# Infini-attention with a SiLU feed-forward: the first query block's mask moved from TensorE to VectorE, and the planned order redrawn

## The chip, the cores and the metric

The kernel runs on one core of a Trainium2 chip. The metric is the device time of one execution in microseconds (us). A core has a matrix engine (TensorE, PE in the profile), with a unit that loads its stationary operand (PEld), a vector engine (VectorE, DVE), an activation engine (ScalarE, ACT), a general engine (GpSimd, POOL) and a queue engine that starts transfers (SyncE, SP). Each engine works through its own instructions in a fixed order, and waits on semaphores where it needs another engine's result. Matrix products land in PSUM, which the kernel uses as eight banks of 128 partitions by 512 fp32.

## The reference

The input `x` has 2048 tokens of width 448. Two branches are mixed by a gate for each token:

```python
q, k, v = x @ wq, x @ wk, x @ wv          # 16 heads of 28, 4 segments of 512 tokens
for s in range(4):                        # for each head
    logits = qs @ ks.T * scale + mask     # causal within the segment
    a_dot = softmax(logits) @ vs
    a_mem = (phi(qs) @ M) / (phi(qs) @ z + 1e-6)
    o = sigmoid(beta) * a_mem + (1 - sigmoid(beta)) * a_dot
    M += phi(ks).T @ vs;  z += phi(ks).sum()
a = concat(o) @ wo
b = silu(x @ w1) @ w2                     # width 1792
g = sigmoid((x * gate_w).sum(-1))
out = g * a + (1 - g) * b
```

`phi` is x + 1 above zero and exp(x) below. `wq` and `wk` come 200 times larger than an ordinary draw, so the softmax needs the true maximum of each row, and the products need more than fp16's precision.

## The kernel before, in words

Each fp32 operand is split into an fp16 part and the fp16 rest, called hi and lo, and a product is made of three products (hi·hi, lo·hi, hi·lo). The work falls into 16 groups, numbered t = 0 to 15: four heads of one segment each.

The first stage, until about 150 us, is `project()`: products for q, k and v (line 632 with `wqs`, `wks`, `wvs`), the sums of the memory M and z (line 1050 and 1052 on TensorE into a `cc` bank; line 1061 on VectorE reduces them into the buffer `md`; line 1064 on GpSimd scales them by `bds` into `macc`; lines 1069 and 1070 make the hi and lo of `macc`), and the retrieval from memory (lines 1087 to 1093). The `bds` and many other scale factors of one to a few columns are made by GpSimd in short instructions (lines 530 and 532), grouped into tasks by a helper, `few`.

The second stage, until about 472 us, mixes two things. One is the attention of 64 heads. For each group, `maxima` first finds the largest score of each row: lines 733 and 737 make scores in an `sc` bank, lines 742 and 747 reduce them on VectorE, line 755 transposes the result. The first query block of a group (128 rows for four heads, 128x512 in one bank) gets its causal mask from TensorE: line 733 multiplies an identity by the mask with start=True, and line 737 adds the four heads' scores on top; line 742 then reduces. For the other blocks line 747 adds the mask and reduces in one instruction. Then, for each head, line 1353 makes the scores again, transposed and with the maximum subtracted; line 1358 (ScalarE) takes exp; lines 1361 and 1364 (GpSimd) clear what lies above the diagonal; line 1370 (ScalarE) makes the hi half; line 1374 (GpSimd, three instructions) makes the lo half; line 1387 (TensorE, 20 matmuls) multiplies by v; line 1395 reduces. The other thing is the feed-forward's first ten of 14 chunks: line 632 with `wa` is the product with W1, lines 1236 and 1237 are a joint pass in which two chunks finish on the two halves of TensorE, lines 1209, 1211, 1213 and 1215 make SiLU and its hi and lo (`ghl`), and line 1257 is the product with W2.

The third stage, until the end, is the rest of the feed-forward and the product with `wo`, which must wait for the attention's output.

What stands where on each engine is decided when the kernel is built, by a list scheduler written in the kernel (`Sched`). It plans each task with a cost (`act`, `dve`, `pool`, `pe`, `few`; `half(512)` is 0.2165 us and `few(n)` is 0.33·n us), a latency from engine to engine, and a priority; among the tasks that can start it takes by priority. Buffers and PSUM banks go round in rings: three banks for `sc`, three for `mm`, two for `cc`, and after the first stage one of `cc`'s goes to `mm`. A task that takes a buffer is planned after its last user. The priorities come from some 35 constants at the head of the file. A planned cost is no instruction: it only moves the task's neighbours. On the chip the instructions keep the planned order and wait for what is late.

Of the names in the excerpts below, `mm_…`, `sc_…` and `cc_…` are tiles in PSUM banks, `mx` holds the maxima, `mk` the mask in fp32, `ring` q and k of a group.

Of the kernel before, what the change touches and what calls it, by code (L numbers as in the profile page):

```python
# [14 lines left out]
OP = mybir.AluOpType  # L15
# [15 lines left out]
TWINP = 30.0  # L31
TWO = 0.27
# [6 lines left out]
MORE = 6  # L39
HPRIO = 26.57  # L40
# [9 lines left out]
WOT = 258.31  # L50
# [3 lines left out]
LOP = 66.17  # L54
LATE = -0.07
FIRST = 104.6
WPRIO = 91.56
MAXO = 57.4
# [3 lines left out]
MP = 23.61  # L62
VF = -52.52
VA = 12.88
VS = 2.68
NV = 8
XH0 = -44.21
NF = 4
VE = 10.92
LASTQ = 6.3  # L70
WQS = -136.22
VH = 44.78
XS0 = -76.47
VC = -7.5
OT1 = -114.26
XS = 34.75
QS = -34.17
KS1 = -32.16
SS = -9.2
# [6 lines left out]
PRICE = 235.91  # L86
PRICE2 = 67.41
SLACK2 = 0.33
PVRUNS = [((1, 0), 1)]
PVP = 79.52  # L90
FLO = 50.28
FHI = 729.09
WOP = 8.33
SZ = 16.64
SZSTEP = 1.72
XPRIO = 345.51
WBP = 34.36
# [183 lines left out]
def infini_mix(ctx: ExitStack, tc: tile.TileContext, x, wq, wk, wv, wo, beta, w1, w2, out):  # L281
# [271 lines left out]
    def others(s, prio, bds, own, t_own, t_gh):  # L553

        def mem():
            z = spk[:, NSEG + s:NSEG + s + 1]
            by(z, top[:, WK:WK + 1], top[:, xi(s)], 1.0 / FIT)
            by(z, z, 1.0 / UP, op0=OP.max)
            by(bds[:, s, :, DH:], own[:, :, None], z[:GW])
            by(bds[:, s, :, :DH], own[:, :, None].to_broadcast([GW, 4, DH]), z[:GW], rv[:GW, s:s + 1])  # L560

        def go():
            by(rv[:, s:s + 1], top[:, WV:WV + 1], top[:, xi(s)], 1.0 / FIT)
            by(omgs[:, s], omg, rv[:, s:s + 1])
# [12 lines left out]
        EREADY[s] = few(5, scores, PREADY[s], SCALED[WQ], SCALED[WK], prio=prio + 0.5)  # L577
        END1.append(EREADY[s])
# [3 lines left out]
    def derive(s, prio):  # L582
# [7 lines left out]
        return few(5, go, SCALED[W1], EREADY[s], GDONE[s], prio=prio)  # L590
# [122 lines left out]
    def maxima(t, o):  # L713
# [12 lines left out]
        for q, (i, hs) in enumerate(plan):  # L726
# [4 lines left out]
            def go(i=i, hs=hs, ps=ps, n=n):  # L731
                if i == 0:
                    nc.tensor.matmul(ps.v, identb, maskb[:, None, :].to_broadcast([128, 4, 128]), start=True,
                                     stop=False, skip_group_check=True)
                for j, hh in enumerate(hs):
                    u = j * n
                    nc.tensor.matmul(ps.v[:, u:u + n], rg.v[:KS, 0, hh, i * 128:(i + 1) * 128], rg.v[:KS, 1, hh, :n],  # L737
                                     start=(i > 0), stop=(i > 0 or j == 3), skip_group_check=(i == 0))

            def red(i=i, hs=hs, ps=ps, n=n):  # L740
                if i == 0:
                    nc.vector.tensor_reduce(mx.v[:, :, 0], ps.v.rearrange("p (h n) -> p h n", h=4), axis=AX.X,
                                            op=OP.max)
                    return
# [4 lines left out]
            m = pe((half(512) if i == 0 else []) + half(n, len(hs)), go, *rs, *MKS, takes=[ps], uses=[rg], prio=p0)  # L749
            reds.append(dve(len(hs) * (n + 184) if i else 512, red, m, *reds[:1], takes=[] if reds else [mx], uses=[ps, mx],  # L750
# [15 lines left out]
    def project():  # L766
# [22 lines left out]
        ring("md", [GW, 4, DH + 1], F32, 1)  # L789
# [59 lines left out]
        def xhalves(s, c, prio):  # L849
# [354 lines left out]
    def unit(s, fs, prio, finish, gate=(), tail=False):  # L1204
# [16 lines left out]
        for a, b in zip(own[::2], own[1::2] + [None]):  # L1221
# [11 lines left out]
            if b is not None:  # L1233
# [4 lines left out]
                m = pe([(TWO, 0.06)], both, *[h[5] for h in held], TWIN[s], uses=[x for h in held for x in (h[1], h[3])],  # L1238
# [304 lines left out]
```

## Time and profile before

| | before |
|---|---|
| median of three runs | 563.09 us (562.89 to 563.65) |
| the profiled execution | 563.36 us, span 561.4 us |
| mean granted clock of TensorE in it | 0.991 |
| busy TensorE, share of the span | 545.4 us, 97% |
| busy ScalarE | 408.7 us |
| busy VectorE | 397.9 us |
| busy GpSimd | 353.9 us |

The profiled execution's time is 1.96 us more than its span, which is the work between the first and the last instruction. In the views, a row gives start, duration, engine, line, operation, output<-input and shape; "x19" are 19 instructions in a row; brackets give the idle time of that engine just before, and what ended it. Matmuls overlap, so the pace of a row of equal ones is its time less one latency, over their count less one.

### The profile page before, as it was taken

Reading aid. Unit: us, or ns where it says so; the run is one execution under the profiler, and the core shown is the slowest. Engines: PE = TensorE matmul, PEld = TensorE weight load, DVE = VectorE, ACT = ScalarE, POOL = GpSimd, SP = SyncE. Lnnn points to the kernel's source line nnn. Section 1 sums busy time; section 2 is a strip of 40 time slices with the busy share of each in tenths; the row PEclk is TensorE's granted clock in tenths of the full one; section 3 lists DMA queues with packets and bytes.
Section 4 is the critical chain, followed back from the end, with each engine's and each line's share of the span. In section 5 each row is a group of like instructions: output and inputs, shape, how many; then the busy total and the mean of one; then the engine's idle time right before and its main releaser. Section 6 shows DMA issues by size and latency. Waiting matters only on the chain.

```text
span 561.4 us, 11595 instructions
## 1 busy us (share of the span) xinstructions
PE 545.4 (97%) x4044; PEld 297.1 (53%) x4044; DVE 397.9 (71%) x987; ACT 408.7 (73%) x700; POOL 353.9 (63%) x550
## 2 busy tenths in 40 slices
PE   9998999899999899999999999999999997999997
PEld 3445655556644455555565555665556553455544
DVE  5998889788668765688655888766885347764472
ACT  6978889576368878899887989789997996500140
POOL 3345354673405787888988988798999996211310
PEclk9999999999999799999999999999999999899999
DMA  8787767453485324322333333456301212689872
GB/s 307 238 242 214 229 192 202 143 179 111 149 225 157 101 60 125 103 84 72 98 94 91 85 87 103 127 143 137 103 19 53 84 51 58 227 210 223 247 190 82
DMA packets 78378, 79.19 MB, mean 141 GB/s; under 512 B 44232, under 2 KB 68040, under 8 KB 78320
## 3 DMA queue, kind: packets, MB, share of 16 engines
q1 hardware_dynamic: 77744, 77.47, 48.1%
q10 hardware_dynamic: 576, 0.99, 0.5%
q8 instruction: 31, 0.51, 0.4%
q14 instruction: 27, 0.22, 0.1%
HBM read 48.41 MB, written 26.09 MB: 133 GB/s over the span
## 4 chain that ended last, share of the span: by engine, by line
PE 63%; DVE 9%; ACT 9%; DMA 8%; POOL 5%; SPq 3%; issue 3%; POOLq 0%; DVEq 0%; ACTq 0%
PE mm L632 16%; PE mm L1257 15%; PE sc L1353 5%; PE sc L737 5%; PE cc L1387 5%; DMA ol<-o_scr 5%; PE sc L632 4%; PE cc L632 4%; PE cc L1257 4%; ACT pf L1358 1%; SPq L657 1%; POOL phl L1374 1%; DVE stg L938 1%; DMA xraw<-in_x_dram 1%; SPq L366 1%
## 5 line engine op out<-in xcount | busy, mean ns | idle before, releaser
L1374 POOL TENSOR_TENSOR phl<-pf,phl 128x384 f16<-128x384 f32 (+1 forms) x192 | 190.5, 1010 | 24.9 <-ACT phl L1370 24.8
L1358 ACT ACTIVATE pf<-sc,lift,es 128x512 f32<-128x512 f32 (+1 forms) x192 | 127.9, 708 | 16.0 <-PE sc L1353 13.6
L747 DVE CUSTOM_DVE_ANT_0 sc<-sc,mk 128x384 f32<-128x384 f32 (+1 forms) x192 | 105.6, 570 | 34.2 <-PE sc L737 32.5
L1257 PE MATMUL mm<-wb,ghl 128*128 128x448 f16 (+2 forms) x516 | 113.7, 352 | 0.0
L632 PE MATMUL mm<-xh,wa 128*128 128x512 f16 x393 | 100.7, 379 | 0.0
L1257 PEld LDWEIGHTS <-ghl 128*128 128x128 f16 x684 | 64.0, 98 | 54.0 <-issue 2.9
L1370 ACT ACTIVATE phl<-pf 128x1280 f16<-128x1280 f32 x64 | 81.3, 1272 | 13.8 <-POOL pf L1364 12.0
L632 PEld LDWEIGHTS <-wa 128*128 128x128 f16 x524 | 48.9, 98 | 52.6 <-issue 7.3
L1353 PE MATMUL sc<-ring 86*128 86x512 f16 (+3 forms) x256 | 62.7, 301 | 1.0 <-DVE mx L747 0.5
L737 PE MATMUL sc<-ring 84*128 84x128 f16 (+3 forms) x256 | 59.4, 303 | 1.1 <-ACT pf L1358 1.1
L1387 PEld LDWEIGHTS <-phl 128*128 128x128 f16 x1280 | 42.0, 96 | 10.8 <-POOL phl L1374 0.7
L643 POOL TENSOR_TENSOR ol<-ol,ml 128x448 f32<-128x448 f32 x12 | 13.8, 1148 | 51.6 <-DMA ol<-o_scr 44.8
L1387 PE MATMUL cc<-vg,phl 128*128 128x29 f16 (+1 forms) x1280 | 44.0, 182 | 0.5 <-POOL phl L1374 0.5
L632 PE MATMUL mm<-xh,wqs 128*128 128x512 f16 x176 | 42.5, 379 | 1.1 <-ACT pp L956 1.1
L632 PE MATMUL mm<-xh,wks 128*128 128x512 f16 x176 | 41.9, 379 | 0.0
L649 ACT ACTIVATE oh<-ol,os 128x448 f16<-128x448 f32 x16 | 10.7, 666 | 42.4 <-POOL ol L643 42.4
L1395 DVE TENSOR_REDUCE oraw<-cc 128x116 f32<-128x232 f32 x64 | 25.3, 396 | 20.6 <-PE cc L1387 20.0
L1257 PE MATMUL cc<-wb,ghl 128*128 128x448 f16 x168 | 39.0, 352 | 0.2 <-DVE ghl L1215 0.2
L632 PE MATMUL cc<-xh,wa 128*128 128x512 f16 x131 | 35.7, 394 | 3.1 <-DVE ghl L1215 3.1
L1353 PEld LDWEIGHTS <-ring 86*128 86x128 f16 x256 | 24.3, 98 | 25.7 <-issue 3.0
L632 PE MATMUL sc<-wos,oT 128*128 128x448 f16 x176 | 35.6, 352 | 0.0
L1364 POOL TENSOR_SCALAR_AFFINE_SELECT pf<-pf 128x384 f32<-128x384 f32 x64 | 33.3, 520 | 2.2 <-ACT pf L1358 1.1
(198 smaller groups left out, 956.3 us busy)
## 6 DMA issues: line engine op xcount, KB each, us to landing
rawf<-in_w_dram SPq DMA_DIRECT2D x26, 256.0 KB
rawf<-in_w_dram SPq DMA_DIRECT2D x28, 224.0 KB
v_scr<-vt SPq DMA_DIRECT2D x16, 232.0 KB
vg<-v_scr SPq DMA_DIRECT2D x16, 232.0 KB
xraw<-in_x_dram SPq DMA_DIRECT2D x14, 256.0 KB
q_scr<-stg SPq DMA_DIRECT2D x16, 224.0 KB
ring<-q_scr SPq DMA_DIRECT2D x16, 224.0 KB
k_scr<-stg SPq DMA_DIRECT2D x16, 224.0 KB
```

Of the source, the lines that this page charges most:

```text
L632: nc.tensor.matmul(ps(), *p[i], start=(i == 0), stop=(i == n - 1 and not more))
L643: d = pool(530, lambda: nc.gpsimd.tensor_add(b.v, b.v, m.v), d, e, uses=[b, m], **k)
L737: nc.tensor.matmul(ps.v[:, u:u + n], rg.v[:KS, 0, hh, i * 128:(i + 1) * 128], rg.v[:KS, 1, hh, :n], start=(i > 0), stop=(i > 0 or j == 3), ...
L747: nc.vector.tensor_tensor_reduce(r, r, MK[:, L - n:], 1.0, NEG, OP.add, OP.max, mx.v[:, hh, i:i + 1])
L1257: nc.tensor.matmul(ps.v[:, lo:hi], g.v[:, y, sl], w.v[:, z, lo:hi], start=(j == 0 and i == 0), stop=(j == len(fs) - 1 and i == 2))
L1353: nc.tensor.matmul(ps.v[:, e:e + w], rg.v[:KK, 1, hh, j * 128:(j + 1) * 128], rg.v[:KK, 0, hh, j * 128:], start=True, stop=True)
L1358: ex.append(sact(e, lambda b=b, ps=ps, pf=pf, e=e: nc.scalar.activation(pf.v[:, b, :e], ps.v[:, :e], AF.Exp, bias=lift, scale=es[:, s:s + ...
L1364: mk.append(pool(204, lambda pf=pf: nc.gpsimd.affine_select(pf.v[:, :, :128], pf.v[:, :, :128], [[0, 3], [1, 128]], OP.is_ge, 0.0, base=0, ...
L1370: hi = copy(1280, lambda hl=hl, flat=flat: nc.scalar.activation(hl.v[:, 0], flat(), AF.Copy), *mk, takes=[hl], uses=[pf], prio=p0 + 2)
L1374: low = pool(w - u + 22, lambda hl=hl, flat=flat, u=u, w=w: nc.gpsimd.tensor_sub(hl.v[:, 1, u:w], flat()[:, u:w], hl.v[:, 0, u:w]), low, u ...
L1387: nc.tensor.matmul(p[:, i, :2 - z], hl.v[:, z, u:u + 128], vg.v[:, j, hh, :2 - z], start=(z == zs[0] and i == 0), stop=(z == zs[-1] and j ...
L1395: nc.vector.tensor_reduce(orw.v[:, hh], p, axis=AX.X, op=OP.add)
```

## The change

Groups 1 to 15 no longer have the product of identity and mask; group 0 keeps it. Their four score products start their bank themselves, and VectorE adds the mask to the bank in place with a `tensor_tensor` of 128x512 before the `tensor_reduce`; the planner counts that task as 1080 columns where it counted 512. The buffer `md` of the memory's sums gets a second copy. The planner counts GpSimd's short tasks as longer (`few`: 7 to 11, 2 to 3, 5 to 10 and 5 to 6), and the joint pass too (`TWO`, 0.27 to 0.33, and its loading part 0.06 to 0.1). One matmul fewer warms TensorE at the start (`MORE`). A transfer for the joint passes, `TWIN`, is given a priority of its own and no longer has to end with the first stage. Some 35 constants of the priorities have new values, so that the order on every engine is another.

```diff
-TWINP = 30.0
-TWO = 0.27
+TWINP = 165.57
+TWO = 0.33
...
-MORE = 6
+MORE = 5
...
-FIRST = 104.6
-WPRIO = 91.56
-MAXO = 57.4
+FIRST = 165.32
+WPRIO = 28.79
+MAXO = 63.55
...
-        PREADY[s] = few(7 if s < NSEG - 1 else 2, go, SCALED[WV], SCALED[NSEG - 1 - s], KREADY.get(s), t_own, t_gh, prio=prio)
+        PREADY[s] = few(11 if s < NSEG - 1 else 3, go, SCALED[WV], SCALED[NSEG - 1 - s], KREADY.get(s), t_own, t_gh, prio=prio)
...
-        EREADY[s] = few(5, scores, PREADY[s], SCALED[WQ], SCALED[WK], prio=prio + 0.5)
+        EREADY[s] = few(10, scores, PREADY[s], SCALED[WQ], SCALED[WK], prio=prio + 0.5)
...
-        return few(5, go, SCALED[W1], EREADY[s], GDONE[s], prio=prio)
+        return few(6, go, SCALED[W1], EREADY[s], GDONE[s], prio=prio)
...
             def go(i=i, hs=hs, ps=ps, n=n):
-                if i == 0:
+                if i == t == 0:
                     nc.tensor.matmul(ps.v, identb, maskb[:, None, :].to_broadcast([128, 4, 128]), start=True,
                                      stop=False, skip_group_check=True)
...
-                                     start=(i > 0), stop=(i > 0 or j == 3), skip_group_check=(i == 0))
+                                     start=i + t > 0, stop=(i + t > 0 or j == 3), skip_group_check=i == t == 0)
...
                 if i == 0:
+                    if t:
+                        r = ps.v.rearrange("p (h n) -> p h n", h=4)
+                        nc.vector.tensor_tensor(r, r, MK[:, None, L - n:].to_broadcast([128, 4, n]), op=OP.add)
...
-            m = pe((half(512) if i == 0 else []) + half(n, len(hs)), go, *rs, *MKS, takes=[ps], uses=[rg], prio=p0)
-            reds.append(dve(len(hs) * (n + 184) if i else 512, red, m, *reds[:1], takes=[] if reds else [mx], uses=[ps, mx],
+            m = pe((half(512) if i == t == 0 else []) + half(n, len(hs)), go, *rs, *MKS, takes=[ps], uses=[rg], prio=p0)
+            reds.append(dve(len(hs) * (n + 184) if i else 1080 if t else 512, red, m, *reds[:1], takes=[] if reds else [mx], uses=[ps, mx],
...
-        ring("md", [GW, 4, DH + 1], F32, 1)
+        ring("md", [GW, 4, DH + 1], F32, 2)
...
-                              prio=prio + TWINP)
-                END1.append(TWIN[s])
+                              prio=TWINP + s)
...
-                m = pe([(TWO, 0.06)], both, *[h[5] for h in held], TWIN[s], uses=[x for h in held for x in (h[1], h[3])],
+                m = pe([(TWO, 0.1)], both, *[h[5] for h in held], TWIN[s], uses=[x for h in held for x in (h[1], h[3])],
```

Two or three added lines move the lines behind them: line 742 of before is 745 after, 747 is 750, 1061 is 1063, 1064 is 1066, 1209 to 1215 are 1211 to 1217, 1353 is 1355, 1387 is 1389.

**The first block of group 5.** On TensorE, before, the product of identity and mask opens the bank `sc_3367`; the score products of the same bank follow (the first of four is shown):

```order
L1353 LDWEIGHTS ring_2135
L1353 MATMUL sc_3363<-ring_2135 128x256
L755 MATMUL sc_3365<-ident,mx 16x128
L733 LDWEIGHTS identb
L733 MATMUL sc_3367<-maskb,identb 128x512
L737 LDWEIGHTS ring_476
L737 MATMUL sc_3367<-ring_476 128x128
```

In the changed kernel the bank, there `sc_3335`, is filled by the four score products alone, and the last of them is followed by the scores of a head and a joint pass:

```order
L737 LDWEIGHTS ring_467
L737 MATMUL sc_3335<-ring_467 128x128
L1355 LDWEIGHTS ring_2133
L1355 MATMUL sc_3340<-ring_2133 128x512
L632 LDWEIGHTS wa
L632 MATMUL mm_3283<-xh_98,wa 128x512
L1238 LDWEIGHTS wa
L1238 MATMUL cc_3243<-xh_98,wa 128x512
```

The pair of line 733 is gone there, and other neighbours stand behind the block.

On VectorE at the same place, before, the bank is read once, by line 742:

```order
L1211 SCALAR_TENSOR_TENSOR mm_3188<-th,mm_3188 128x512
L1211 SCALAR_TENSOR_TENSOR cc_3253<-th,cc_3253 128x512
L742 TENSOR_REDUCE mx<-sc_3367 128x4
L759 SCALAR_TENSOR_TENSOR mhl_3381<-sc_3365,mhl_3381 16x128
L1215 SCALAR_TENSOR_TENSOR ghl<-mm_3188,ghl 128x512
```

After, the mask is added (line 744) and then the bank is reduced (line 745):

```order
L750 ISA sc_3324,mx<-sc_3324,mk 128x512
L750 ISA mx 128x1
L1217 SCALAR_TENSOR_TENSOR ghl<-mm_3084,ghl 128x512
L744 TENSOR_TENSOR sc_3335<-sc_3335,mk 128x512
L745 TENSOR_REDUCE mx<-sc_3335 128x4
L1217 SCALAR_TENSOR_TENSOR ghl<-mm_3151,ghl 128x512
```

One instruction more stands in VectorE's row, and the rest of `mm_3151` waits behind both.

**The end of the attention.** On TensorE, before, this stands behind the last product of the last head (`cc_7179`); `cc_7235` is the next tile in the bank that `cc` gave to `mm`, which `cc_7051` holds until its `ghl` is made:

```order
L1387 MATMUL cc_7179<-vg,phl 128x58
L632 LDWEIGHTS wa
L632 MATMUL mm_7163<-xh_99,wa 128x512
L1236 LDWEIGHTS wa
L1236 MATMUL mm_7146<-xh_99,wa 128x512
L1237 LDWEIGHTS wa
L1237 MATMUL mm_7163<-xh_99,wa 128x512
L632 LDWEIGHTS wa
L632 MATMUL cc_7235<-xh_99,wa 128x512
```

After, four products for `mm_7154`, ten for `mm_7198` (the first of each is shown) and the joint pass stand between the last product of the last head (`cc_7165`) and `cc_7235`:

```order
L1389 MATMUL cc_7165<-vg,phl 128x58
L632 MATMUL mm_7154<-xh_99,wa 128x512
L632 MATMUL mm_7198<-xh_99,wa 128x512
L1238 LDWEIGHTS wa
L1238 MATMUL mm_7154<-xh_99,wa 128x512
L1239 LDWEIGHTS wa
L1239 MATMUL mm_7198<-xh_99,wa 128x512
L632 LDWEIGHTS wa
L632 MATMUL cc_7235<-xh_99,wa 128x512
```

Fourteen products stand there in place of one.

On VectorE, before, what releases that bank is the last line 1215 here, for `cc_7051`:

```order
L1395 TENSOR_REDUCE oraw<-cc_7123 128x116
L595 SCALAR_TENSOR_TENSOR wb<-rawf,up,wb 128x448 x2
L1286 SCALAR_TENSOR_TENSOR th<-th,hsum 128x512
L1277 TENSOR_TENSOR hsum<-hl 128x512
L595 SCALAR_TENSOR_TENSOR ghl<-th,hso,ghl 128x512
L1395 TENSOR_REDUCE oraw<-cc_7179 128x116
L1399 RECIPROCAL rl<-oraw 128x16
L595 SCALAR_TENSOR_TENSOR wb<-rawf,up,wb 128x448
L1211 SCALAR_TENSOR_TENSOR cc_7051<-th,cc_7051 128x512
L1211 SCALAR_TENSOR_TENSOR mm_7103<-th,mm_7103 128x512
L1215 SCALAR_TENSOR_TENSOR ghl<-cc_7051,ghl 128x512
```

After, it is line 1217 for `cc_7080`:

```order
L1213 SCALAR_TENSOR_TENSOR mm_7036<-th,mm_7036 128x512
L595 SCALAR_TENSOR_TENSOR wb<-rawf,up,wb 128x448
L595 SCALAR_TENSOR_TENSOR ghl<-th,hso,ghl 128x512
L1217 SCALAR_TENSOR_TENSOR ghl<-mm_7036,ghl 128x512
L1397 TENSOR_REDUCE oraw<-cc_7165 128x116
L1401 RECIPROCAL rl<-oraw 128x16
L1213 SCALAR_TENSOR_TENSOR cc_7080<-th,cc_7080 128x512
L1213 SCALAR_TENSOR_TENSOR mm_7129<-th,mm_7129 128x512
L1217 SCALAR_TENSOR_TENSOR ghl<-cc_7080,ghl 128x512
```

The `wb` that stood between the reciprocal and the bank's first line 1211 now stands ahead of the reduction of the last head.

**The first sums of the memory.** On GpSimd, before, two runs of short instructions for other scale factors stand between the last `bds` and the first `macc`:

```order
L532 TENSOR_SCALAR bds<-of,spk,rv 112x4x28
L532 TENSOR_SCALAR es<-top 128x1
L532 TENSOR_SCALAR es<-top,es 128x1
L532 TENSOR_SCALAR wide<-top 64x1 x2
L530 TENSOR_SCALAR wide<-wide 128x1
L1064 TENSOR_TENSOR macc<-md,bds 112x116
L1070 TENSOR_TENSOR mhl<-macc,mhl 112x116
L1064 TENSOR_TENSOR macc<-md,bds 112x116
```

(The four rows of `es` and `wide` stand there twice.) After, the first `macc` comes right behind `bds`:

```order
L532 TENSOR_SCALAR bds<-of,spk,rv 112x4x28
L1066 TENSOR_TENSOR macc<-md,bds 112x116
L532 TENSOR_SCALAR es<-top 128x1
L532 TENSOR_SCALAR es<-top,es 128x1
L532 TENSOR_SCALAR wide<-top 64x1 x2
L530 TENSOR_SCALAR wide<-wide 128x1
L1072 TENSOR_TENSOR mhl<-macc,mhl 112x116
L1066 TENSOR_TENSOR macc<-md,bds 112x116 x2
L1072 TENSOR_TENSOR mhl<-macc,mhl 112x116 x2
```

On VectorE, in the changed kernel, the two sums `cc_584` and `cc_606` go to `md` one behind the other:

```order
L940 SCALAR_TENSOR_TENSOR stg<-mm_486,stg 128x512
L1063 TENSOR_REDUCE md<-cc_584 112x116
L1063 TENSOR_REDUCE md<-cc_606 112x116
L960 TENSOR_SCALAR pp<-mm_486,tqk 112x512
L940 SCALAR_TENSOR_TENSOR stg<-mm_534,stg 128x512
```

Before, three other instructions of VectorE stood between the first two.

More of the change, by code (lines that the diff above doesn't have):

```diff
@@ L38 @@
 WARM = 8
-MORE = 6
-HPRIO = 26.57
+MORE = 5
+HPRIO = 13.32
 BANKS = {"mm": 3, "sc": 3, "cc": 2}
@@ L49 @@
 FIT = 2.0 ** -15
-WOT = 258.31
+WOT = 154.32
 TUS = 1.6
@@ L53 @@
 SLACK = -0.5
-LOP = 66.17
+LOP = 35.82
 LATE = -0.07
-FIRST = 104.6
-WPRIO = 91.56
-MAXO = 57.4
+FIRST = 165.32
+WPRIO = 28.79
+MAXO = 63.55
 FULL = 0.111
@@ L61 @@
 RB = "cc"
[L62 to L65, printed above, removed]
+MP = 24.27
+VF = -54.82
+VA = 12.33
+VS = 0.91
 NV = 8
-XH0 = -44.21
+XH0 = -75.6
 NF = 4
[L69 to L73, printed above, removed]
-VC = -7.5
[L75 to L79, printed above, removed]
+VE = 6.18
+LASTQ = 6.73
+WQS = -122.17
+VH = 29.33
+XS0 = -34.76
+VC = -7.5
+OT1 = -143.04
+XS = 35.55
+QS = -29.35
+KS1 = -24.75
+SS = -14.29
 def VP(o, k):
     return o + VA + VS * k if o or k > VF else -1.0 + 0.1 * k
-PRICE = 235.91
-PRICE2 = 67.41
-SLACK2 = 0.33
+PRICE = 267.48
+PRICE2 = 150.04
+SLACK2 = 0.15
 PVRUNS = [((1, 0), 1)]
[L90 to L97, printed above, removed]
+PVP = 86.58
+FLO = 41.44
+FHI = 709.77
+WOP = 85.61
+SZ = 13.48
+SZSTEP = 0.12
+XPRIO = 324.18
+WBP = 27.13
 XLEAD = 146.82
```

## The prediction

> **What bounds the kernel now.** I read the page first, then the waits of TensorE, then windows around the places where its granted clock falls. The page's busy times:
>
> ```profile
> PE 545.4 (97%) x4044; PEld 297.1 (53%) x4044; DVE 397.9 (71%) x987; ACT 408.7 (73%) x700; POOL 353.9 (63%) x550
> PEclk9999999999999799999999999999999999899999
> ```
>
> TensorE is busy for 545.4 of 561.4 us; no other engine passes 73%. So the time is TensorE's work, plus its idle time (16 us), plus what two dips of the clock cost. The waits of TensorE say whom it idles for (us in all, times, longest):
>
> ```profile
> PE cc L632 <- DVE ghl L1215: 3.1, 1, 3.1
> PE sc L980 <- DVE sums L474: 1.6, 1, 1.6
> PE mm L632 <- ACT pp L956: 1.1, 1, 1.1
> PE sc L737 <- ACT pf L1358: 1.1, 2, 0.9
> PE sc L1353 <- DVE mx L747: 0.5, 1, 0.5
> PE sc L1353 <- DVE mx L742: 0.2, 1, 0.2
> ```
>
> One wait of 3.1 us leads, then a few of about one. No queue is short again and again; the gains lie in single places. The windows give stretch, length, busy time of PE, PEld, DVE, ACT and POOL, granted clock, DMA share, GB/s:
>
> ```profile
> 183.08:186.49 3.41, 2.55 (x33) 1.61 (x33) 2.88 (x12) 3.41 (x7) 2.49 (x4) 1.00 0.29 75
> 186.49:193.32 6.83, 5.77 (x16) 2.21 (x16) 5.71 (x14) 5.32 (x8) 5.47 (x7) 0.50 0.49 124
> 194.00:470.00 276.00, 275.31 (x2575) 155.68 (x2573) 185.54 (x527) 240.43 (x355) 244.49 (x339) 1.00 0.32 88
> 473.20:476.62 3.42, 0.43 (x3) 0.19 (x2) 3.16 (x6) 2.23 (x5) 1.47 (x2) 1.00 0.26 86
> 476.62:480.03 3.41, 3.41 (x10) 1.22 (x9) 3.27 (x6) 2.25 (x4) 1.15 (x1) 0.51 1.01 314
> ```
>
> From 194 to 470 us TensorE idles 0.69 us in 276, so there only fewer products help, and VectorE has 90 us to spare (185.5 of 276). The clock is halved for 6.83 us at 186.5 and for 3.41 us at 476.6; work done at half speed takes twice its time, so these cost about 2.9 (half of the 5.77 busy) and 1.7 us.
>
> The sum is made against the profiled execution's 563.36 us, 0.27 above the median of the runs (563.09). I call 0.2% (1.1 us) what a measurement can tell from no change.
>
> **The masks leave TensorE.** The products of line 733, and the pace of 512-column products in a full row:
>
> ```profile
> L733 PE MATMUL sc<-maskb,identb 128*128 128x512 bf16 x16 | 6.1, 379 | 0.0
> 467.72 4.26 PE L632 MATMUL mm<-xh,wa 128*128 128x512 f16 x19
> ```
>
> 379 ns is one product's latency. The pace is (4.26 − 0.38)/18 = 0.216 us, and that is what a removed product frees in a full queue. Fifteen go: 15 × 0.216 = 3.24 us off, nearly all in the stretch without idle time.
>
> **The masks come to VectorE.** No row shows the very instruction. The nearest are the reduction of the same bank, line 742 (minimum, median, maximum in ns), and an addition of the same size out of SBUF:
>
> ```profile
> L742 DVE TENSOR_REDUCE mx<-sc x16: 670/682/693, 53.1 to 426.1; 128x4 f32<-128x512 f32 x16
> L1277 DVE TENSOR_TENSOR hsum<-hl x2: 684/688/691, 471.1 to 491.9; 128x512 f32<-128x512 f16 x2
> ```
>
> I take 0.69 us; 15 × 0.69 = 10.3 us more on VectorE, lifting it from 67% to about 72% of that stretch. What is queued behind each: line 745, then the `ghl` and the line 747 of the next block; who waits is the scores' bank. Counted in the planned order with each product at its pace, TensorE's work between the block's last product and the next use of its bank was 1.5 to 2.6 us before (once 0.4), and is 2.05 to 3.1 us after. The chain that must fit is 0.68 us before and 0.69 + 0.68 = 1.37 us after. So the slack is at least 0.68 us in each group, the length of one more instruction ahead in VectorE's row; a second one makes TensorE wait 0.7 us. Ends: 0, and a wait for the whole addition in every group, 10.3 us. I take three groups in fifteen at 0.69, +2.1 us, nearer the low end, since 0.69 us is all that the stretch loses today.
>
> **The memory's first sums.** Here GpSimd, VectorE and TensorE wait in a chain (start, duration, work, idle time before):
>
> ```profile
> 37.98 2.61 POOL L530 TENSOR_SCALAR bds<-of,spk 112x4 f32<-112x4 f32 x1
> ...
> 43.94 0.26 POOL L532 TENSOR_SCALAR es<-top 128x1 f32<-128x1 f32 x1
> ...
> 46.98 0.22 POOL L530 TENSOR_SCALAR wide<-wide 128x1 f32<-128x1 f32 x1
> 47.16 0.43 POOL L1064 TENSOR_TENSOR macc<-md,bds 112x116 f32<-112x116 f32 x1
> 47.62 0.40 DVE L1061 TENSOR_REDUCE md<-cc 112x116 f32<-112x232 f32 x1 [1.81 <-POOL macc L1064]
> 49.95 0.57 PE L980 MATMUL sc<-ident,ph 112*128 112x112 f32 x4 [1.62 <-DVE sums L474]
> ```
>
> GpSimd's short run ends at 47.2; the only `md` is held until the first `macc` is done; the second sum waits 1.81 us on VectorE with everything behind it, and TensorE 1.62 us. With two buffers the second sum needs no `macc`, and in the new order the two stand in a row; GpSimd's `es` and `wide` go behind the first `macc`, some 3.2 us (43.9 to 47.2) earlier. So −1.6. A third sum still waits for the first buffer, and the exact wait of the next consumer can't be read from the order: ends −1.8 and +1.
>
> **The end of the attention.** The largest wait, seen from ScalarE, VectorE and TensorE:
>
> ```profile
> 468.23 2.24 DVE L595 SCALAR_TENSOR_TENSOR wb<-rawf,up,wb 128x448 f16<-128x448 f32 x2
> 473.56 0.61 DVE L595 SCALAR_TENSOR_TENSOR wb<-rawf,up,wb 128x448 f16<-128x448 f32 x1
> 474.09 0.69 DVE L1211 SCALAR_TENSOR_TENSOR cc<-th,cc 128x512 f32<-128x512 f32 x1
> 475.44 0.69 DVE L1215 SCALAR_TENSOR_TENSOR ghl<-cc,ghl 128x512 f16<-128x512 f32 x1
> 471.82 0.68 PE L1387 MATMUL cc<-vg,phl 128*128 128x29 f16 x20
> 472.65 0.39 PE L1237 MATMUL mm<-xh,wa 64*128 64x512 f16 x1
> 476.19 4.22 PE L632 MATMUL cc<-xh,wa 128*128 128x512 f16 x11 [3.15 <-DVE ghl L1215]
> ```
>
> From the last head's product (471.82) to the bank's release (476.19) it is 4.37 us, and TensorE has one product and a joint pass to fill them. After, the `wb` of 473.56 stands ahead of this chain, so it should be some 0.5 us shorter, 3.9 us; and fourteen products and the joint pass, 13 × 0.216 = 2.8 us more, stand in the gap. With 3.15 us of wait before, 3.15 − 0.5 − 2.8 leaves nothing: the wait goes, and with it the half clock at 476.6, 3.15 + 1.7 = 4.85. I take −4.7, since the total is close to the edge; ends −4.9 and 0 (if the chain is later by as much). What is late next is line 1257, which needs the `ghl` of the last chunks: about 5.7 us of products stand in front of it.
>
> **The crowd at 184.** The row of waits where the stages meet:
>
> ```profile
> 184.59 0.38 PE L1353 MATMUL sc<-ring 86*128 86x512 f16 x1 [0.22 <-DVE mx L742]
> 185.51 0.38 PE L1353 MATMUL sc<-ring 86*128 86x384 f16 x2 [0.54 <-DVE mx L747]
> 187.58 0.48 PE L737 MATMUL sc<-ring 84*128 84x384 f16 x1 [0.87 <-ACT pf L1358]
> 188.24 0.59 PE L737 MATMUL sc<-ring 84*128 84x512 f16 x1 [0.19 <-ACT pf L1358]
> ```
>
> The `sc` banks turn too fast here: the scores of a head and the blocks of line 737 come together with no feed-forward products between. The two windows above show 0.86 and 1.06 us of idle time; giving each product the pace of its size, TensorE falls some 3 us behind there (an estimate), and it runs 6.83 us of it at half clock. In the new order there are two such crowds, six and seven takes of an `sc` bank in little more than 2 us each; worked through with the rows' durations they lose 3.7 us. So +0.7, the half clock as before. Ends: −5.9 (3.0 and 2.9 both gone) and +3.6 (the second crowd halves the clock once more, 2.9, on top of the 0.7).
>
> [...]
>
> **At nothing.** The planner's longer costs of the joint pass and of GpSimd's work change no instruction. The warm matmul taken away lies at the start, where TensorE waits for data. The same number of transfers starts on SP; `TWIN`'s are moved behind the first stage's others, where the joint pass alone waits for them. GpSimd's and ScalarE's counts change by an instruction or four out of hundreds.
>
> Sum: −3.24 + 2.1 − 1.6 − 4.7 + 0.7 = −6.74, so 563.36 − 6.74 = 556.6 us.
>
> **Rivals.**
>
> First, the waits move. The order is new everywhere, and each of the single waits can come back at another place, with its dip of the clock. For it: VectorE ends the largest waits, and it gets 10.3 us more work. Against: the order shows the causes of the two largest gone. Then the terms of −1.6 and −4.7 fall out, and 563.36 − 3.24 + 2.1 + 0.7 = 562.9 us: no change that can be told.
>
> Second, slower: the banks held longer. If VectorE has two or more instructions ahead of each addition, TensorE waits for the addition in every group: 10.3 in place of 2.1 gives 556.6 + 8.2 = 564.8; if such short idle times also bring the clock down in two of the groups, as the crowd at 184 did (2.9 each), 570.6. It decides where the waits of the fifteen groups pass 0.59 us on average, (6.74 + 2.1)/15. For it: line 747 alone puts 105.6 us on VectorE, in bursts around these blocks:
>
> ```profile
> L747 DVE CUSTOM_DVE_ANT_0 sc<-sc,mk 128x384 f32<-128x384 f32 (+1 forms) x192 | 105.6, 570 | 34.2 <-PE sc L737 32.5
> ```
>
> Against: its 34.2 us of idle time end with the very product of line 737, so there VectorE mostly waits for TensorE, not the other way. [...]
>
> Third, the crowds come apart: the redrawn order spreads the blocks at the stage's start, and its waits and half clock go as well. Then 556.6 − 0.7 − 5.9 = 550.0. Against it: the takes counted above.
>
> **How the numbers follow.** My forecast, with its own range of 553 to 560, gets 0.45. The first rival gets 0.20, half of it at 560 to 562 (faster), the rest mostly within 0.2%; the second 0.20, nearly all slower; the third 0.15. Faster: 0.45 + 0.15 + 0.10 = 0.70; same 0.08; slower 0.22. The range for 8 in 10 runs from the third rival's 550.0 to 566.5, just above the second's 564.8; below lie some 0.07, above some 0.13.
>
> **What would show it.** The waits of TensorE should have no row of 3 us for line 632 behind `ghl`, and the clock after the last head should stay at 1.00. The second `md` should come within 0.1 us of the first, with no idle time behind `macc`. Line 744 should show 15 instructions of about 0.69 us, and the stretch from 194 to 470 should take about 3 us less for the same heads and no more than 3 us of waits for lines 745 and 750. If that stretch loses 7 us or more, or the clock dips in it, the prediction is wrong by the second rival; if the wait at the attention's end stands, by the first.

## The result, and the profile after

The changed kernel takes 549.42 us (median of 4, 548.73 to 550.8) against 562.99 us of the kernel before (median of 4, 562.2 to 563.65): a ratio of 0.9763, 95% interval 0.9739 to 0.9787. It is 13.6 us faster. The direction was forecast, and the size was not: the prediction was 556.6 us with a range from 550.0, so the result lies below the range, at twice the gain.

The page of the profiled execution (550.8 us, the longest of the four; span 549.0), busy time and granted clock:

```profile
PE 538.8 (98%) x4028; PEld 295.7 (54%) x4028; DVE 408.9 (74%) x1005; ACT 406.3 (74%) x696; POOL 354.0 (64%) x552
PEclk9999999999998999999999999999999999999999
```

Between the two profiled executions the span falls by 12.4 us. TensorE's busy time gives 6.6 of it (545.4 to 538.8) and its idle time 5.8 (16.0 to 10.2). Busy time holds the fifteen products and the clock: there is one dip (0.55 for 3.4 us) where there were two (0.50 for 6.83 us, 0.51 for 3.41). Five of the waits of TensorE:

```profile
PE mm L814 <- DVE sums L830: 1.0, 1, 1.0
PE sc L1355 <- DVE mx L750: 1.0, 3, 0.5
PE cc L632 <- DVE ghl L1217: 0.9, 1, 0.9
PE sc L737 <- DVE mx L745: 0.7, 1, 0.7
PE sc L982 <- DVE ph L965: 0.3, 1, 0.3
```

The 3.1 us behind the last `ghl` and the 1.6 of line 980 behind `sums` are gone, and what is left is small. The first row is old: the kernel before has it too, at 1.0 us. Of the others only the 0.7 us behind line 745 is a wait for a bank that is held longer. The 1.0 us behind line 750 is no such wait, as the run a_mask_pe shows below. By stage, the kernel before and then the changed one (stretch, length, busy time of PE, PEld, DVE, ACT, POOL, clock, DMA share, GB/s):

```profile
30.00:160.00 130.00, 124.57 (x737) 71.85 (x735) 109.78 (x236) 92.86 (x205) 66.28 (x142) 1.00 0.63 184
160.00:194.00 34.00, 32.09 (x187) 14.84 (x186) 27.98 (x69) 27.73 (x44) 17.39 (x21) 0.90 0.60 162
194.00:440.00 246.00, 245.31 (x2301) 139.42 (x2299) 173.57 (x507) 214.79 (x317) 215.63 (x301) 1.00 0.34 93
440.00:484.00 44.00, 40.85 (x338) 21.29 (x337) 24.07 (x40) 34.74 (x55) 32.61 (x43) 0.96 0.33 106
```

```profile
30.00:160.00 130.00, 129.11 (x763) 74.97 (x762) 114.45 (x245) 93.39 (x206) 66.27 (x140) 1.00 0.66 195
160.00:194.00 34.00, 31.22 (x220) 15.49 (x219) 29.68 (x78) 28.75 (x45) 20.59 (x26) 0.95 0.47 131
194.00:440.00 246.00, 244.65 (x2305) 138.95 (x2302) 180.17 (x511) 217.82 (x322) 223.44 (x313) 1.00 0.34 95
440.00:484.00 44.00, 43.89 (x326) 22.42 (x324) 30.04 (x48) 31.72 (x50) 25.20 (x31) 1.00 0.38 123
```

Idle time is length less the first busy time. It goes from 5.43 to 0.89 us in the first stage, from 1.91 to 2.78 where the stages meet, from 0.69 to 1.35 among the heads, and from 3.15 to 0.11 at the attention's end. The first of these is the surprise.

The added instruction costs nearly what was estimated, 0.70 us in the median where 0.69 was taken (minimum, median and maximum in ns):

```profile
L744 DVE TENSOR_TENSOR sc<-sc,mk x15: 676/700/731, 162.5 to 410.2; 128x512 f32<-128x512 f32 x15
```

### The profile page after: what moved, and what is told of

Its sections match the earlier page's. It is cut to its first block, busy times and chain, and to the rows that moved or that the text cites. A ratio compares the mean times of both kernels' runs of the same rounds, so it can differ in the third digit from the quotient of the medians.

```text
span 549.0 us, 11601 instructions
## 1 busy us (share of the span) xinstructions
PE 538.8 (98%) x4028; PEld 295.7 (54%) x4028; DVE 408.9 (74%) x1005; ACT 406.3 (74%) x696; POOL 354.0 (64%) x552
## 4 chain that ended last, share of the span: by engine, by line
PE 72%; ACT 8%; DMA 6%; DVE 6%; POOL 4%; issue 2%; SPq 1%; DVEq 0%; POOLq 0%; ACTq 0%
PE mm L632 18%; PE mm L1259 17%; PE sc L632 10%; PE cc L1259 6%; PE sc L737 5%; PE sc L1355 5%; PE cc L1389 5%; PE cc L632 3%; ACT pf L1360 3%; DMA rawf<-in_w_dram 2%; POOL phl L1376 2%; ACT phl L1372 1%; DMA k_scr<-stg 1%; DMA xraw<-in_x_dram 1%; PE cc L1089 1%
## 5 line engine op out<-in xcount | busy, mean ns | idle before, releaser
L1259 PE MATMUL mm<-wb,ghl 128*128 128x448 f16 (+2 forms) x516 | 111.9, 348 | 0.1
L737 PE MATMUL sc<-ring 84*128 84x128 f16 (+3 forms) x256 | 57.2, 300 | 1.6 <-DVE mx L745 0.7
L643 POOL TENSOR_TENSOR ol<-ol,ml 128x448 f32<-128x448 f32 x12 | 13.6, 1132 | 49.7 <-DMA ol<-o_scr 39.2
```

The source lines that it names most:

```text
L643: d = pool(530, lambda: nc.gpsimd.tensor_add(b.v, b.v, m.v), d, e, uses=[b, m], **k)
L1259: nc.tensor.matmul(ps.v[:, lo:hi], g.v[:, y, sl], w.v[:, z, lo:hi], start=(j == 0 and i == 0), stop=(j == len(fs) - 1 and i == 2))
```

## The experiments

Each kernel is compared with the kernel before in the same session by its ratio; 0.001 is 0.56 us. There are two kinds. In the first, the order on every engine is that of one of the two kernels, and one thing in it is exchanged. In the second, numbers of the planner are exchanged, which alter no instruction's work, and the order is drawn anew.

**The masks, in both orders.** The changed kernel's order, with the masks on TensorE again (a_mask_pe):

```diff
-                if i == t == 0:
+                if i == 0:
                     nc.tensor.matmul(ps.v, identb, maskb[:, None, :].to_broadcast([128, 4, 128]), start=True,
...
-                    if t:
-                        r = ps.v.rearrange("p (h n) -> p h n", h=4)
-                        nc.vector.tensor_tensor(r, r, MK[:, None, L - n:].to_broadcast([128, 4, n]), op=OP.add)
```

> The changed kernel with its own order on every engine, but the masks of groups 1 to 15 again made by TensorE's product (15 products of line 733 back, 15 additions of line 744 gone). Theory: most of the gain comes from the new order; the products alone cost 15 x 0.216 = 3.2 us, less up to 2.1 us of waits behind the longer held banks: 550.5 to 552.7 us. Rival: moving the masks is what brings the gain, since the first blocks' products and what waits for them stand in TensorE's full stretch: 555 us or more.

It took 552.07 us, a ratio of 0.9815 (0.9792 to 0.9838): 0.0052 or 2.9 us above the changed kernel's ratio, and the two intervals don't meet. So in that order the move of the masks is worth 2.9 us of the 13.6, near the 3.24 of its products. The wait of 0.7 us for the reduction of the first block is gone from the list; the waits for the other blocks stay as they were (line 747 of this kernel is line 750 of the changed one):

```profile
PE sc L1352 <- DVE mx L747: 0.9, 3, 0.5
160.00:194.00 34.00, 32.16 (x232) 16.22 (x230) 28.45 (x76) 28.99 (x47) 21.83 (x28) 0.95 0.48 132
194.00:440.00 246.00, 244.82 (x2294) 138.80 (x2293) 169.65 (x496) 215.73 (x318) 221.38 (x311) 1.00 0.35 94
```

With the masks back on TensorE it idles 1.84 us where the stages meet (2.78 in the changed kernel) and 1.18 us among the heads (1.35). What the longer held banks cost in this order is therefore some 1 us. Most of it is one wait in group 1, in the changed kernel:

```profile
163.98 0.34 PE L737 MATMUL sc<-ring 84*128 84x384 f16 x1 [0.74 <-DVE mx L745]
```

The same move in the order before (b_mask_dve; the reverse of the diff above, planned costs untouched):

> The kernel before with its own order, but the masks of groups 1 to 15 added by VectorE. Theory (order): 3.2 us of products go, and 1 to 3 us of waits come, since the next use of the bank stands only 1.5 us behind the block in many groups: 560.5 to 562.5 us. Rival, the prediction's second (banks held longer stop TensorE in every group): 566 us or more. Rival (the mask alone brings half of the gain): 557 us or less.

It took 564.99 us, 1.0057 (1.0034 to 1.0079): 3.2 us slower than before, between the theory and the slow rival. The products are gone, and more has come (line numbers are 3 higher than before, so 1356 is 1353):

```profile
PE sc L1356 <- DVE mx L745: 3.1, 5, 1.0
PE sc L737 <- DVE mx L745: 0.5, 1, 0.5
```

The weight loads ahead of these matmuls wait too, and more often (who waited for line 745: us, times):

```profile
  PEld L1356: 6.5, 10
  PE sc L1356: 3.1, 5
  PEld L737: 0.9, 1
```

A load and its matmul can wait for the same thing at the same time, so these rows are not to be added up: in the changed kernel's trace the load and the product of line 737 that both start at 163.98 us waited 1.03 and 0.74 us, both for line 745. The 3.2 us hold more than waits: eleven of this kernel's twelve executions had a granted clock of 0.991, while the 23 of the kernel before went up to 1.000. At 0.991 the medians are 564.6 and 563.1 us, a loss of 1.5 us; whether the additions also made the low clock more frequent is not shown. What is sure is the sign: the same fifteen additions gain 2.9 us in the changed order and lose 1.5 to 3.2 in the order before. By the count of the prediction, the products between the block's last one and the next use of its bank take 1.5 to 2.6 us in the order before, and 2.05 to 3.1 in the changed one. That this gap decides is an argument from that count; no run alters the gap alone. It fits that the largest stall is in group 2, the one where the gap was 0.4 us:

```profile
186.48 0.39 PE L1356 MATMUL sc<-ring 86*128 86x512 f16 x1 [0.96 <-DVE mx L745]
```

**The second md, in both orders.** The order before, with a second buffer for `md` while the planner still counts one (b_md2):

```diff
-        ring("md", [GW, 4, DH + 1], F32, 1)
+        R["md"] = Ring(1, lambda: wp.tile([GW, 4, DH + 1], F32, name="md", bufs=2))
```

> The kernel before with its own order, but two copies of md. The prediction's step: the second sum no longer waits 1.8 us on VectorE and TensorE's wait of 1.6 us at 50 us goes: 561.2 to 561.8 us. Theory (order): part of that wait comes back at the next instruction that stands behind the late macc: 562 to 563 us. Rival (the second buffer clears the whole first stage): 558 us.

It took 561.79 us, 0.9999 (0.9976 to 1.0022): no change. VectorE's wait for `macc` did go: the second reduction stands at 45.59, not at 47.62. And TensorE's wait of 1.6 us for `sums` stayed, because another chain from the same late `macc` ends at the same time (VectorE, then ScalarE, of this kernel):

```profile
45.59 0.38 DVE L1061 TENSOR_REDUCE md<-cc 112x116 f32<-112x232 f32 x1
45.90 0.67 DVE L938 SCALAR_TENSOR_TENSOR stg<-mm,stg 128x512 f16<-128x512 f32 x1
48.33 0.68 DVE L985 SCALAR_TENSOR_TENSOR phk<-sc,spk,phk 128x448 f16<-128x448 f32 x1 [1.76 <-ACT phk L983]
...
47.48 0.30 ACT L1069 ACTIVATE mhl<-macc 112x116 fp32r<-112x116 f32 x1 [2.46 <-POOL macc L1064]
47.68 0.62 ACT L983 ACTIVATE phk<-sc,spk 128x448 f16<-128x448 f32 x1
```

ScalarE stands 2.46 us in front of `mhl`, with the next `phk` queued behind it; VectorE then waits 1.76 us for that `phk` in place of 1.81 for `macc`. The changed kernel's order with one buffer (a_md1; the line that takes the buffer away is shown, and the rest of the edit emits the plan so that each engine keeps its order):

```diff
-        ring("md", [GW, 4, DH + 1], F32, 2)
+        R["md"] = sch.md = Ring(2, lambda: wp.tile([GW, 4, DH + 1], F32, name="md", bufs=1))
```

> The changed kernel with its own order on every engine, but one copy of md again. Theory (order): the second sum waits for the first macc, some 0.6 us on VectorE, of which little reaches TensorE: 549.4 to 550.4 us. Rival (the second buffer is what clears the first stage, which gained some 5 us): 552 to 555 us.

It took 550.79 us, 0.9781 (0.9757 to 0.9805). This is 1.0 us above the changed kernel, within what the two intervals allow as none. VectorE waits 0.99 us for `macc` there, but TensorE's idle time from 30 to 160 us is 0.91 us, as with two buffers (0.89). The second buffer is not the gain of the first stage.

**macc earlier on GpSimd alone.** The order before (b_es_late), in which the first `macc` and its lo go ahead of the two runs of `es` and `wide`:

```diff
+        EREADY[s].late = s < 2
...
+            lo.first_lo = t == 0
...
+            if getattr(t, "late", False):
+                held.append(t)
+                continue
...
+            if held and getattr(t, "first_lo", False):
+                for h in held:
+                    h.fn()
```

> The kernel before with its own order on TensorE, VectorE, ScalarE and SyncE; on GpSimd alone the first macc and its lo go ahead of the two runs of es and wide. Theory: the late macc holds up ScalarE's mhl and what stands behind it as well as the second md, so that TensorE's wait of 1.6 us near 50 us goes only when macc itself comes earlier: the wait of L980 for sums is under 0.4 us, and the time is 1 to 2 us below the kernel before. Rival: this wait has yet another cause behind it: the wait stays over 1 us and the time is that of the kernel before.

It took 563.03 us, 1.0022 (1.0003 to 1.0042): no gain, where the theory had 1 to 2 us. The wait for `sums` at 50 us is gone, as the theory had it, but `es` and `wide` now stand between the first `macc` and the second, and the stop is there (GpSimd, ScalarE, VectorE of this kernel, whose lines are 15 higher):

```profile
49.60 0.43 POOL L1079 TENSOR_TENSOR macc<-md,bds 112x116 f32<-112x116 f32 x1
...
50.06 0.30 ACT L1084 ACTIVATE mhl<-macc 112x116 fp32r<-112x116 f32 x1 [2.82 <-POOL macc L1079]
...
51.55 0.69 DVE L953 SCALAR_TENSOR_TENSOR stg<-mm,stg 128x512 f16<-128x512 f32 x1 [2.40 <-ACT pp L971]
```

The changed kernel escapes this in another way: there ScalarE's first `mhl` stands so far back in its row that it comes 4 us after `macc`, and nothing queues behind a wait (GpSimd, then ScalarE):

```profile
46.10 0.43 POOL L1066 TENSOR_TENSOR macc<-md,bds 112x116 f32<-112x116 f32 x1 [0.22 <-DVE md L1063]
...
50.18 0.61 ACT L985 ACTIVATE phk<-sc,spk 128x448 f16<-128x448 f32 x1
50.70 0.29 ACT L1071 ACTIVATE mhl<-macc 112x116 fp32r<-112x116 f32 x1
50.89 0.58 ACT L938 ACTIVATE stg<-mm 128x512 f16<-128x512 f32 x1
```

**The planned lengths and the constants, drawn anew.** The kernel before with the longer planned costs alone (b_few):

```diff
-        PREADY[s] = few(7 if s < NSEG - 1 else 2, go, SCALED[WV], SCALED[NSEG - 1 - s], KREADY.get(s), t_own, t_gh, prio=prio)
+        PREADY[s] = few(11 if s < NSEG - 1 else 3, go, SCALED[WV], SCALED[NSEG - 1 - s], KREADY.get(s), t_own, t_gh, prio=prio)
...
-        EREADY[s] = few(5, scores, PREADY[s], SCALED[WQ], SCALED[WK], prio=prio + 0.5)
+        EREADY[s] = few(10, scores, PREADY[s], SCALED[WQ], SCALED[WK], prio=prio + 0.5)
...
-        return few(5, go, SCALED[W1], EREADY[s], GDONE[s], prio=prio)
+        return few(6, go, SCALED[W1], EREADY[s], GDONE[s], prio=prio)
```

> The kernel before with the longer planned costs of GpSimd's short tasks alone (7 to 11, 2 to 3, 5 to 10, 5 to 6), so planned anew; the instructions are the same. Theory (truer lengths clear the first stage): TensorE's idle time from 30 to 112 us falls from 5.4 to 2 us or less, and the time is 3 to 5 us below the kernel before. Rival (the redrawn constants clear it): the waits move but stay at 4 us or more there; the time is within 2 us of the kernel before, on either side.

It took 557.97 us, 0.9923 (0.9901 to 0.9945), 4.3 us faster, as the theory had it. TensorE's idle time from 30 to 112 us is 1.15 us (5.43 before):

```profile
30.00:112.00 82.00, 80.85 (x490) 47.68 (x489) 77.63 (x175) 68.93 (x158) 45.72 (x97) 1.00 0.73 214
```

The longer costs do not bring `macc` earlier. GpSimd still runs `es` and `wide` ahead of it, and it starts at 46.86 us (47.16 before). Its readers stand further back: ScalarE's first `mhl` comes at 52.52 with no idle time in front of it, and so does VectorE's second sum at 52.12 (GpSimd, then ScalarE of this kernel):

```profile
46.86 0.43 POOL L1064 TENSOR_TENSOR macc<-md,bds 112x116 f32<-112x116 f32 x1
...
52.52 0.28 ACT L1069 ACTIVATE mhl<-macc 112x116 fp32r<-112x116 f32 x1
```

Nor are the longer costs truer throughout. In the kernel before one run of `es` and `wide` takes 1.6 us (43.94 to 45.53), which the planner counted as 1.65 and counts as 3.3 now; only the runs that end in `bds` were counted too short (4.9 and 2.9 us against 2.31; now 3.63).

The changed kernel with the shorter costs (a_few_old; the diff reversed):

> The changed kernel with the old, shorter planned costs of GpSimd's short tasks (11 to 7, 3 to 2, 10 to 5, 6 to 5), so planned anew. Theory (truer lengths): 3 to 5 us above the changed kernel, with waits behind GpSimd's scale factors back in the first stage. Rival (the constants): within 2 us of the changed kernel.

It took 560.02 us, 0.9976 (0.9953 to 0.9999): 12 us above the changed kernel, more than the theory had, and in the wrong place. From 30 to 160 us it idles 1.64 us, which is little. Among the heads it idles 3.58 us, 2.2 more than the changed kernel, and the mean clock where the stages meet is 0.90 (0.95 there), which over the 34 us costs some 1.7 us more (an estimate from the two clocks):

```profile
30.00:160.00 130.00, 128.36 (x752) 73.74 (x751) 113.72 (x242) 94.13 (x207) 67.22 (x141) 1.00 0.64 188
160.00:194.00 34.00, 31.19 (x198) 14.50 (x197) 25.82 (x67) 26.13 (x41) 18.21 (x22) 0.90 0.52 142
194.00:440.00 246.00, 242.42 (x2256) 136.49 (x2254) 186.43 (x525) 215.48 (x318) 212.59 (x299) 1.00 0.35 94
```

The kernel before with the changed kernel's constants alone (b_consts; the core of the diff):

```diff
-FIRST = 104.6
-WPRIO = 91.56
-MAXO = 57.4
+FIRST = 165.32
+WPRIO = 28.79
+MAXO = 63.55
...
-PRICE = 235.91
-PRICE2 = 67.41
+PRICE = 267.48
+PRICE2 = 150.04
```

> The kernel before with the changed kernel's constants of the priorities alone; planned costs, masks and md as before (the joint pass at 0.27, TWINP and MORE as before). Theory (the constants hold the gain only together with the planned lengths for which they were drawn): within 3 us of the kernel before. Rival (the constants alone hold it): 6 to 9 us below the kernel before.

It took 559.61 us, 0.9953 (0.9937 to 0.9969), 2.6 us faster, so the theory holds (within 3 us). The wait at the end of the attention is gone, and the idle time among the heads is 3.75 us in place of 0.69:

```profile
194.00:440.00 246.00, 242.25 (x2258) 137.00 (x2257) 176.34 (x508) 215.69 (x320) 212.27 (x298) 1.00 0.34 93
440.00:484.00 44.00, 44.00 (x363) 23.16 (x362) 22.58 (x41) 34.69 (x53) 31.08 (x40) 1.00 0.41 132
```

**What any redraw does.** A single constant is moved by a hundredth or two, for which there is no reason but to draw the order anew; between a quarter and a third of TensorE's rows move. Two from the changed kernel (a_va, a_first), two from the kernel before (b_va, b_wprio):

```diff
-VA = 12.33
+VA = 12.45
```

> The changed kernel with one constant of the priorities one hundredth larger (VA, 12.33 to 12.45), which redraws a quarter of TensorE's order and changes no instruction. Theory (the changed kernel's order is a rare draw in which single waits fit together): 2 to 8 us above the changed kernel. Rival (the gain is in the planned costs, the masks and md, and any near order has it): within 1.5 us of the changed kernel.

```diff
-FIRST = 165.32
+FIRST = 168.63
```

> The changed kernel with another constant two hundredths larger (FIRST, 165.32 to 168.63), which redraws a quarter of TensorE's order and changes no instruction. Theory (a rare draw): 2 to 8 us above the changed kernel. Rival: within 1.5 us of it.

```diff
-VA = 12.88
+VA = 13.01
```

> The kernel before with one constant one hundredth larger (VA, 12.88 to 13.01), which redraws a third of TensorE's order and changes no instruction. Theory (each redraw moves single waits of one to three us and dips of the clock): 1 to 6 us away from the kernel before, more likely above it. Rival (a redraw alone does little): within 1 us of it.

```diff
-WPRIO = 91.56
+WPRIO = 93.39
```

> The kernel before with another constant two hundredths larger (WPRIO, 91.56 to 93.39), which redraws a third of TensorE's order and changes no instruction. Theory: 1 to 6 us away from the kernel before, more likely above it. Rival: within 1 us of it.

| kernel | time, us | ratio to before | 95% interval |
|---|---|---|---|
| changed | 549.42 | 0.9763 | 0.9739 to 0.9787 |
| a_va | 561.28 | 0.9971 | 0.9944 to 0.9998 |
| a_first | 557.48 | 0.9892 | 0.9862 to 0.9921 |
| b_va | 559.17 | 0.9916 | 0.9889 to 0.9944 |
| b_wprio | 558.64 | 0.9937 | 0.9911 to 0.9963 |

Both redraws of the changed kernel lose, 12 and 7 us. Both redraws of the kernel before move it by 3.5 and 4.7 us, and downwards, which was not expected to be the likelier side. So the changed kernel's order is a better one than its neighbours, the one before was not, and a difference of 4 us, b_few's too, can't by itself be credited to the number that was altered.

**The lengths, in pairs.** For that reason three more draws of above, with the planned lengths alone exchanged by b_few's diff or its reverse (b_wprio_few, a_va_few_old, a_first_few_old):

> The kernel before with WPRIO at 93.39 and the longer planned costs of GpSimd's short tasks. Theory (truer lengths clear the first stage under any draw): TensorE's idle time from 30 to 160 us falls from the 4.5 us of the same draw with the short costs to 2 us or less. Rival (b_few was one draw among others): it stays at 3 us or more. The whole time may go either way by the draw.

> The changed kernel with VA at 12.45 and the old, shorter planned costs. Theory: TensorE's idle time from 30 to 160 us rises from 1.3 us to 3 us or more. Rival: it stays under 2 us. The whole time may go either way by the draw.

> The changed kernel with FIRST at 168.63 and the old, shorter planned costs. Theory: TensorE's idle time from 30 to 160 us rises from 0.6 us to 3 us or more. Rival: it stays under 2 us. The whole time may go either way by the draw.

TensorE's idle time from 30 to 160 us, in us, from the same row of each profile:

| same draw of the other numbers | short lengths | long lengths |
|---|---|---|
| before | 5.43 | 2.00 |
| before, WPRIO at 93.39 | 4.46 | 1.68 |
| changed | 1.64 | 0.89 |
| changed, VA at 12.45 | 0.76 | 1.34 |
| changed, FIRST at 168.63 | 0.81 | 0.61 |

Two of the rows, of the kernel before with WPRIO at 93.39, with the short and then with the long lengths:

```profile
30.00:160.00 130.00, 125.54 (x742) 72.53 (x741) 109.77 (x238) 94.53 (x207) 67.51 (x141) 1.00 0.65 189
```

```profile
30.00:160.00 130.00, 128.32 (x753) 73.40 (x751) 113.73 (x241) 94.58 (x206) 70.01 (x141) 1.00 0.65 191
```

With the settings of before, the longer lengths take 2.8 and 3.4 us of waits out of the first stage in two draws of two; the theory holds there. With the changed kernel's other settings the stage is clear either way, and the rival holds. So two things clear it, each without the other: the longer planned lengths, or the rest of the changed settings. Which of that rest does it stays open: its constants alone leave 3.13 us (b_consts), and what was not taken apart is the planned second `md`, `TWIN`, `TWO` and the masks' planned cost. In all seventeen kernels the stage goes with one wait. In the six that idle 3.8 us or more there (before, b_mask_dve, b_md2, b_es_late, b_va, b_wprio) ScalarE stands 2.4 to 2.8 us in front of one of the first two `mhl`, waiting for `macc`; in the eleven others, which idle 3.13 us or less, no such wait passes 0.54 us. As whole times, the three took 558.39 us (0.9908), 558.27 (0.9922) and 553.13 (0.9818, 0.9772 to 0.9863): the last is the lowest of all redraws, with the short lengths, and 4 us below the same draw with the long ones.

## Why the prediction was wrong

- **The masks leave TensorE** (−3.24, with +2.1 of waits on VectorE's side): the mechanism was right and the waits were overrated. At one order the move gives −2.9. The one wait behind line 745 is 0.74 us, in group 1, where three of 0.69 were taken, so the slack that was counted held in fourteen groups of fifteen. Idle time among the heads, from 194 to 440, rose by 0.66 us, but 0.49 of that is there with the masks on TensorE too (1.18 against 0.69) and comes from the order.
- **The memory's first sums** (−1.6): this is the step that failed, in size and in mechanism. The stage lost 4.5 us of idle time, not 1.6. The sum took up one row of the list of waits, and left the other rows of the first stage at nothing, without a reason, though the order there is drawn anew as everywhere else. Besides the 1.1 us for `pp` that the prediction shows, the kernel before has these, and smaller ones:

```profile
PE cc L476 <- DVE amr L1093: 0.8, 1, 0.8
PE sc L980 <- DVE ph L963: 0.7, 1, 0.7
```

  And the row that it took was read one step short: the wait of VectorE for `macc` was on the chain, but so was ScalarE's for `mhl`, of nearly the same length beside it. With two buffers and nothing else the time is the same (b_md2). What the cleared orders share is that ScalarE no longer waits so long for `macc`. In b_few and in the changed kernel that is because its `mhl` stands further back. Which of the settings beside the planned lengths does this stays open.
- **The end of the attention** (−4.7): right. Idle time there fell by 3.04 us, and the clock of the stretch from 440 to 484 us rose from 0.96 to 1.00, which is the 1.7 us of the dip. In b_consts, drawn with the new constants and without the rest, the idle time there is gone too, and the clock is 1.00.
- **The crowd at 184** (+0.7): the idle time where the stages meet is +0.87 us, which looks as counted, but by luck. 0.74 of it is the wait of group 1 for its mask, ahead of the crowds; with the masks on TensorE the same order idles 1.84 us there, against 1.91 before. So the two new crowds cost TensorE about as much idle time as the old one, not more. The clock differs: it is halved in one stretch of 3.4 us, not in 6.83, which gives some 1.7 us that the step did not have (an estimate, from 0.95 against 0.90 over the 34 us; the last section says how far such a dip belongs to the order):

```profile
171.90:175.30 3.40, 2.10 (x12) 0.95 (x11) 2.79 (x7) 3.40 (x6) 1.79 (x2) 0.95 0.91 242
175.30:178.70 3.40, 3.40 (x11) 1.30 (x10) 3.21 (x6) 3.40 (x5) 1.84 (x4) 0.55 0.08 30
```

- **The sum from the traces**: −3.24 (products) − 4.54 (first stage) − 3.04 − 1.7 (attention's end) + 0.87 − 1.7 (where the stages meet) + 0.66 (heads) = −12.7, against −12.4 of the span and −6.74 forecast. Of the difference of some 6 us, half (2.9) is the first stage, 1.7 the clock at the crowds, and the rest the waits that were taken for the masks and the crowd.
- **The rivals.** The first (the waits move) is what happens in four of the five other orders of the changed kernel's instructions: they idle 3.17 to 3.58 us among the heads (1.35 in the changed kernel, 1.38 in a_first_few_old, which is the fastest of the five). The second, slower, is real in the order before, though smaller than it was priced: there the same additions cost 1.5 to 3.2 us more than they save. The third gave a time, 550.0, that is nearly the measured one, by the wrong cause: the crowds did not come apart, and the nearness of its number is luck.
- **The range** put the lower bound at the one rival with a lower time and gave the redrawn order no spread of its own. The changed kernel's instructions alone, under six orders, measured from 549 to 561 us here. That spread, not the sum of the terms, was the largest uncertainty.

## What to carry to other kernels

When a planner sets the order, price the instructions that change at a fixed order (keep the order and exchange them), and measure a few redraws without meaning before crediting a gain to a number of the planner: here such redraws moved the time by 3.5 to 12 us, up to nearly as much as the whole change. Of two waits that ended at the same late producer, taking one away was worth nothing here (the second `md` alone: a ratio of 0.9999), so follow each producer to all its readers, on every engine. Moving work off the busiest engine can gain or lose with the order (here it gained 2.9 us in one and lost 1.5 to 3.2 in the other): count the gap up to the next use of the buffer that is held longer, and try the move in the order that you mean to keep.

## What the runs showed of the hardware

In these runs the half clock does not follow from the idle time in a stretch alone, nor from the order. From 160 to 194 us the kernel before idles 1.91 us and its clock is 0.90; the same order with the second `md` idles 2.31 us, and its clock stays at 1.00 (the row of that kernel):

```profile
160.00:194.00 34.00, 31.69 (x215) 15.32 (x214) 29.07 (x72) 28.48 (x46) 16.86 (x22) 1.00 0.60 165
```

So dips come or don't on nearly the same work. They also come and go in one and the same kernel. The 86 executions of the kernel before that the experiments list have a mean granted clock of 0.988 to 1.000 and times of 558.1 to 566.6 us; the three at 1.000 took 558.1 to 559.1 us, and the six at 0.997 have a median of 560.2. The changed kernel's four executions all show 0.997. At that clock the gain is therefore some 10.8 us (an estimate across sessions, 560.2 to 549.4); the rest of the 13.6 goes with how often the dips come. That the new order itself makes them rarer is the author's estimate, from the wait of 3.15 us that is gone together with the 0.51 behind it; no run shows it.

Of the warm products at the start, the first eight (line 811 before) took 634 ns in the median, the six behind them (line 816, `MORE`) 384; in the changed kernel it is 634 and, for five, 379. The granted clock of the first 4.4 us reads 1.00 in both. Whether the first ones make the later ones faster is not shown: no run leaves them out.
